# Turning u for the channel layers: by TensorE, or by the transposing DMA in 16-bit halves

## The chip, the cores and the metric

The kernel runs on one core of a Trainium2 chip. The metric is the device time of one execution in microseconds (us), as the median of three runs. A profiled run beside them gives the trace and a page of tables; its span, from the first to the last instruction, is 864.8 us.

The engines of the core work side by side and meet through semaphores: TensorE (PE in the tables, its weight loads PEld), VectorE (DVE), ScalarE (ACT), GpSimd (POOL), and SyncE (SP), which here issues nearly all transfers. A line number such as L584 is a line of the kernel before.

## The reference

Two blocks in a row: routed attention, then a mixer with a token layer and a channel layer. Only the second matters here.

```python
def _moe_ref(x, w_tok1, w_tok2, w_ch1, w_ch2):     # x: (4, 768, 512), the attention's output
    xt = x.transpose(0, 2, 1)
    h = np.maximum(xt @ w_tok1, 0.0) @ w_tok2      # w_tok1: (768, 256), w_tok2: (256, 768)
    u = x + h.transpose(0, 2, 1)
    h2 = np.maximum(u @ w_ch1, 0.0) @ w_ch2        # w_ch1: (512, 1536), w_ch2: (1536, 512)
    return (u + h2).astype(np.float32)
```

All arrays are fp32. `u` has 768 tokens by 512 channels for each of 4 batches.

## The kernel before

In SBUF, `xs[b]` holds u of batch b with tokens on the 128 partitions: `[128, 6, 512]`, six blocks of 128 tokens. The product `u @ w_ch1` sums over channels, so it needs u with channels on the partitions. That is what `turn_u` makes: `uT`, in two halves of 384 tokens (n) by four blocks of 128 channels (f). Each of the eight (n, f) blocks takes three transposes of 128x128 on TensorE into PSUM, and one copy to SBUF, on ScalarE and VectorE in turn.

```python
def turn_u(b, n):
    if n == 0:
        pools["uT"] = pools["u"].tile([P, 2, NF, HS], F32, name="uT")       # HS = 384, NF = 4
        pools["uTs"] = pools["u"].tile([P, 3, NF // 2, HS], F32, name="uTs")
    uT, uTs = pools["uT"], pools["uTs"]
    for f in range(NF):
        pt = pools["ps_m"].tile([P, HJ, P], F32, tag="YZ"[f % 2], name="pt")
        for i in range(HJ):                                                  # HJ = 3
            nc.tensor.transpose(                                             # L584
                out=pt[:, i], in_=xs[b][:, HJ * n + i, f * P : (f + 1) * P], identity=ident
            )
        copy = nc.vector.tensor_copy if f % 2 else nc.scalar.copy
        copy(out=uT[:, n, f], in_=pt.rearrange("p i t -> p (i t)"))          # L588
    if n == 1:
        R = {"B11": uT[:, 0, 0:2], "B21": uT[:, 0, 2:4], "B22": uT[:, 1, 2:4]}
        R["T1"], R["T2"], R["T4"] = (uTs[:, i] for i in range(3))
        R["T3"] = b12 = uT[:, 1, 0:2]
        sub(R["T1"], b12, R["B11"])          # on VectorE, 128x768 each, L535
        sub(R["T2"], R["B22"], R["T1"])
        sub(R["T3"], R["B22"], b12)
        sub(R["T4"], R["B21"], R["T2"])
        pools["R"] = R
```

The sums T1 to T4 are there because both channel layers use the seven-product scheme of Strassen and Winograd: a chunk of a layer is seven products over blocks and sums of blocks instead of eight over blocks.

```python
def chunk(n, product, done, last=False):
    X = ptile("X")
    product(X, "A11", "B11", True)
    if late:
        late.pop()()                     # the last product of the chunk before (A22, T4; c21)
    done("p1", X)                        # first layer: ScalarE copies X to SBUF
    Z = ptile("Z")
    product(Z, "S1", "T1", True)
    done("p5", Z)                        # first layer: ScalarE copies Z
    Y = ptile("Y")
    ...                                  # product(Y, "A12", "B21", True); done("c11", Y)
    product(X, "S2", "T2", False)        # accumulates onto X, which must have been copied
    done("u2", X)
    ...                                  # product(Z, "S4", "B22", False); done("c12", Z)
    product(X, "S3", "T3", False)
    done("c22", X)
    ...                                  # product(X, "A22", "T4", False); done("c21", X): put into late
```

`done` adds on VectorE and, in the first layer (`ch1_chunk`, products at L656), copies (L664) and takes the relu (L668, L675, L688) on ScalarE; in the second (`ch2_chunk`, products at L707) all of it is on VectorE (L538). `ptile` has two buffers for each of X, Y and Z.

The main loop over batches, and the token layers (`ends`, L512 and L521) ahead of it, between which the first batch is turned:

```python
while ends:                               # products of the token layers, with weight work beside them
    ...
    ends.pop(0)()
    if len(ends) in (11, 9):
        turn_u(0, len(ends) == 9)
...
for b in range(B):
    for part in range(2):
        for i in range(3):
            ch1_chunk(part, i)
            ...
        for i in range(3):
            ...
            ch2_chunk(b, part, i)
            if part == 1 and i < 2 and b + 1 < B:
                turn_u(b + 1, i)
        ...
```

Of the kernel before, what the change touches and what calls it, by code (L numbers as in the profile page):

```python
# [8 lines left out]
F32 = mybir.dt.float32  # L9
BF16 = mybir.dt.bfloat16  # L10
U32 = mybir.dt.uint32
I32 = mybir.dt.int32
ALU = mybir.AluOpType
ACT = mybir.ActivationFunctionType
# [2 lines left out]
B, H, S, D = 4, 8, 768, 64  # L17
C = 16
P = 128
NJ = S // P  # L20
DM = H * D
NF = DM // P
# [4 lines left out]
HJ = NJ // 2  # L27
HS = HJ * P
# [19 lines left out]
def kernel(  # L48
# [29 lines left out]
    nc = tc.nc  # L78
# [30 lines left out]
    pools = {}  # L109


    ident = const.tile([P, P], F32, name="ident")
# [15 lines left out]
    xs = [xpool.tile([P, NJ, DM], F32, name=f"x{b}") for b in range(B)]  # L128
# [51 lines left out]
    def weight_steps(pool, W, names):  # L180
# [8 lines left out]
        def tmp(name, dt, n):  # L189
            bufs = 1 if name == "wT" else 2  # L190
            return pool.tile([P, WMAX], dt, tag=name, name=name, bufs=bufs)[:, 0:n]

        def load_bits(src, p):
            n = p["n"] = src.shape[1]
            raw = pool.tile([P, WMAX, 2], U32, tag="raw", name="raw", bufs=3)[:, 0:n]
            nc.sync.dma_start(raw.rearrange("p n two -> p (n two)"), src.bitcast(U32))
            p["lo"], p["hi"] = raw[:, :, 0], raw[:, :, 1]

        def scalar_part(p):

            p["h"] = tmp("wh", U32, p["n"])
            nc.scalar.activation(out=p["h"].bitcast(F32), in_=p["hi"].bitcast(F32), func=ACT.Abs)
            p["up"] = tmp("wup", I32, p["n"])
            nc.scalar.activation(out=p["up"], in_=p["lo"], func=ACT.Copy, scale=float(2.0**-29))

        def rest(dst, p):
# [10 lines left out]
            )  # L217
            T = tmp("wT", U32, p["n"])
            nc.vector.scalar_tensor_tensor(  # L219
                out=T, in0=p["hi"], scalar=0xC0000000, in1=h,  # L220
                op0=ALU.bitwise_and, op1=ALU.bitwise_or,
            )
            T, up = T.bitcast(I32), p["up"]
            if len(dst.shape) == 3:
                T, up = (y.rearrange("t (p j) -> t p j", j=NJ) for y in (T, up))
            nc.gpsimd.tensor_tensor(out=dst.bitcast(I32), in0=T, in1=up, op=ALU.add)  # L226

# [15 lines left out]
    def centroids_norm(cen):  # L243
# [9 lines left out]
        nc.vector.tensor_scalar(  # L253
            out=nrm.bitcast(I32), in0=lo.bitcast(I32), scalar1=0.5, scalar2=float(0x1FBB6875),
            op0=ALU.mult, op1=ALU.add,
# [251 lines left out]
    def tok1(b, t):  # L507
        if t == 0:
            h1s[b] = tokpool.tile([P, NT, DM], F32, name="h1", bufs=2)
        pf = mtile([P, DM], "ph1")  # L510
        for j in range(NJ):
            nc.tensor.matmul(  # L512
                pf, lhsT=W["tok1"][:, j, t * P : (t + 1) * P], rhs=xs[b][:, j],
                start=(j == 0), stop=(j == NJ - 1),
            )
        relu(h1s[b][:, t], pf)
# [17 lines left out]
    def sub(dst, a, b):  # L534
        nc.vector.tensor_tensor(out=dst, in0=a, in1=b, op=ALU.subtract)  # L535

    def add(dst, a, b):
        nc.vector.tensor_tensor(out=dst, in0=a, in1=b, op=ALU.add)  # L538

    def left_weights():  # L540

        w = W["ch1"]
        half = DCH // 2
        A = {
            f"A{i + 1}{j + 1}": w[:, 2 * j : 2 * j + 2, half * i : half * i + half]
            for i in range(2)
            for j in range(2)
        }
        extra = pools["wsums"].tile([P, 3, 2, half], F32, name="w1s")
        A["S1"], A["S2"], A["S4"] = (extra[:, i] for i in range(3))  # L550
        yield lambda: add(A["S1"], A["A21"], A["A22"])
        yield lambda: sub(A["S2"], A["S1"], A["A11"])
        yield lambda: sub(A["A21"], A["A11"], A["A21"])
        yield lambda: sub(A["S4"], A["A12"], A["S2"])
        A["S3"] = A["A21"]
        pools["A"] = A
# [15 lines left out]
        B_["T3"] = B_["B12"]  # L572
        pools["B"] = B_

    def turn_u(b, n):

        if n == 0:
            pools["uT"] = pools["u"].tile([P, 2, NF, HS], F32, name="uT")
            pools["uTs"] = pools["u"].tile([P, 3, NF // 2, HS], F32, name="uTs")
        uT, uTs = pools["uT"], pools["uTs"]  # L580
        for f in range(NF):
            pt = pools["ps_m"].tile([P, HJ, P], F32, tag="YZ"[f % 2], name="pt")
            for i in range(HJ):
                nc.tensor.transpose(  # L584
                    out=pt[:, i], in_=xs[b][:, HJ * n + i, f * P : (f + 1) * P], identity=ident
                )
            copy = nc.vector.tensor_copy if f % 2 else nc.scalar.copy
            copy(out=uT[:, n, f], in_=pt.rearrange("p i t -> p (i t)"))  # L588
        if n == 1:
            R = {"B11": uT[:, 0, 0:2], "B21": uT[:, 0, 2:4], "B22": uT[:, 1, 2:4]}  # L590
            R["T1"], R["T2"], R["T4"] = (uTs[:, i] for i in range(3))
            R["T3"] = b12 = uT[:, 1, 0:2]
            sub(R["T1"], b12, R["B11"])
            sub(R["T2"], R["B22"], R["T1"])
            sub(R["T3"], R["B22"], b12)
            sub(R["T4"], R["B21"], R["T2"])
            pools["R"] = R

    late = []

# [42 lines left out]
    def ch1_chunk(part, i):  # L643

        c = 3 * part + i
        if i == 0:
            pools["h2"] = {
                k: pools["mlp"].tile([P, 3, HS], F32, name="h" + k)
                for k in ("A11", "A12", "A22", "S1", "S2", "S3", "S4")
            }  # L650
        A, R, h2 = pools["A"], pools["R"], pools["h2"]
        kept = {}

        def product(psum, a, r, start):
            for k in range(2):
                nc.tensor.matmul(  # L656
                    psum, lhsT=A[a][:, k, c * P : (c + 1) * P], rhs=R[r][:, k],
                    start=start and k == 0, stop=k == 1, skip_group_check=not start,
                )

        def done(name, psum):
            if name in ("p1", "p5", "u2"):
                kept[name] = pools["mlp"].tile([P, HS], F32, name=name, bufs=2)
                nc.scalar.copy(out=kept[name], in_=psum)  # L664
            elif name == "c11":
                a = h2["A11"][:, i]
                add(a, psum, kept["p1"])
                nc.scalar.activation(out=a, in_=a, func=ACT.Relu)  # L668
            elif name == "c12":
                kept["c12"] = pools["mlp"].tile([P, HS], F32, name="c12", bufs=2)  # L670
                add(kept["c12"], psum, kept["u2"])
            elif name == "c22":
                a = h2["A22"][:, i]
                add(a, psum, kept["p5"])
                nc.scalar.activation(out=a, in_=a, func=ACT.Relu)  # L675

                nc.vector.scalar_tensor_tensor(
                    out=h2["S3"][:, i], in0=kept["c12"], scalar=0.0, in1=h2["A11"][:, i],
                    op0=ALU.max, op1=ALU.subtract,
                )  # L680
                nc.vector.scalar_tensor_tensor(
                    out=h2["S1"][:, i], in0=kept["c12"], scalar=0.0, in1=a,
                    op0=ALU.max, op1=ALU.add,
                )
                sub(h2["S2"][:, i], h2["S1"][:, i], h2["A11"][:, i])
            else:
                a = h2["A12"][:, i]
                nc.scalar.activation(out=a, in_=psum, func=ACT.Relu)  # L688
                sub(h2["S4"][:, i], a, h2["S2"][:, i])

        chunk(HS, product, done)
# [34 lines left out]
    good = const.tile([P, 3], F32, name="good")  # L726
    count = const.tile([1, 3], I32, name="count")

# [77 lines left out]
    ends = [lambda t=t: tok1(0, t) for t in range(NT)]  # L806
# [73 lines left out]
    pools["wsums"] = pool("wsums", 1, side="right")  # L880
    pools["u"] = pool("upool", 1, side="right")
    beside = weights + list(left_weights())
    while ends:
        for _ in range(-(-len(beside) // len(ends))):
            beside.pop(0)()
        ends.pop(0)()
        if len(ends) in (11, 9):
            turn_u(0, len(ends) == 9)
    staging.close()
    tokens.close()  # L890
    pools["mlp"] = pool("mlp", 1)
# [1 line left out]
    for b in range(B):  # L893
        for part in range(2):
            for i in range(3):
                ch1_chunk(part, i)
                for _ in range(2):
                    if beside:
                        beside.pop(0)()
            for i in range(3):  # L900
                if b == B - 1 and part == 1 and i == 2:
                    both = fits_load()
                ch2_chunk(b, part, i)
                if part == 1 and i < 2 and b + 1 < B:
                    turn_u(b + 1, i)
            if b == 0:
                (fits_count if part else fits)()
    late.pop()()
# [212 lines left out]
```

## Time and profile before

| | us |
|---|---|
| device time, median of three runs | 867.04 (866.88 to 867.43) |
| span of the profiled run | 864.8 |
| TensorE clock granted | 0.998 of full speed |

The stages, read from the trace: attention up to about 330 us, the token layers up to 416 us, and the channel layers of four batches from there to the end. The groups of instructions that turn u (columns: line, engine, operation, out<-in, shape, count; then busy us in all and mean ns of one; then the idle time of the engine just before them and what ended it):

```profile
L584 PE MATMUL pt<-ident,x 128*128 128x128 f32 x96 | 11.8, 273 | 0.0
L588 DVE COPY uT<-pt 128x384 f32<-128x384 f32 x16 | 8.9, 558 | 2.2 <-PE pt L584 1.4
L588 ACT COPY uT<-pt 128x384 f32<-128x384 f32 x16 | 7.7, 480 | 53.1 <-PE pt L584 53.1
L535 DVE TENSOR_TENSOR uTs<-uT,uTs 128x768 f32<-128x768 f32 x8 | 7.6, 955 | 0.4
```

The mean of one transpose, 273 ns, includes the fill of a pipeline in which neighbours overlap; what twelve of them take on the path is read from the chain of work that ended last, in order of time. Busy time is the union of an engine's instructions. An engine's idle time costs something only where the engine is on that chain.

### The profile page before, as it was taken

What the parts mean: (1) busy time and instruction counts of PE and PEld (TensorE: products, weight loads), DVE (VectorE), ACT (ScalarE), POOL (GpSimd) and SP (SyncE); (2) the same over time, 40 slices, a digit from 0 to 9 for tenths busy, and PEclk for the clock granted to TensorE, in tenths of its full rate; (3) what the DMA queues carried; (4) which work ended last, traced back from release to release, by engine and by line L of the source; (5) the groups of instructions that cost most, each with busy time, mean ns of one, the idle gap of its engine ahead of it and who ended that gap; (6) DMA issues with size and microseconds to landing.
All of it is one profiled execution on the core that took longest, in us unless ns stands there. A gap on an engine that the chain in (4) does not pass through costs nothing.

```text
span 864.8 us, 11041 instructions
## 1 busy us (share of the span) xinstructions
PE 856.0 (99%) x4294; PEld 525.0 (61%) x4294; DVE 511.0 (59%) x864; ACT 290.7 (34%) x490; POOL 45.8 (5%) x40
## 2 busy tenths in 40 slices
PE   9999999999999999999999999999999999999997
PEld 4444444444444444445578586685876867768676
DVE  6878887989898861896553444423444334443342
ACT  5566566566666651321210311203112021120210
POOL 1001010101101000330000000000000000000000
PEclk9999999999999999999999999999999999999999
DMA  9855455666564300420000010000010000100001
GB/s 148 150 122 114 92 116 112 126 99 137 113 128 105 87 25 0 145 75 1 0 1 1 0 38 37 0 1 0 25 49 1 0 1 25 49 1 1 0 14 64
DMA packets 133276, 47.62 MB, mean 55 GB/s; under 512 B 122080, under 2 KB 126176, under 8 KB 133216
## 3 DMA queue, kind: packets, MB, share of 16 engines
q1 hardware_dynamic: 131616, 46.45, 24.2%
q8 instruction: 35, 0.57, 0.3%
q10 hardware_dynamic: 1600, 0.39, 0.2%
q14 instruction: 25, 0.20, 0.1%
HBM read 34.64 MB, written 6.29 MB: 47 GB/s over the span
## 4 chain that ended last, share of the span: by engine, by line
PE 94%; DVE 4%; issue 0%; DMA 0%; DVEq 0%; ACT 0%
PE sc L420 18%; PE pX L707 14%; PE pX L656 14%; PE av L443 14%; PE pZ L707 7%; PE pZ L656 7%; PE ph L512 4%; PE pY L707 4%; PE pY L656 4%; PE pu L521 3%; PE px L472 1%; PE small L459 1%; PE pt L584 1%; PE small L301 1%; DVE wh L214 1%; DVE wT L219 1%
## 5 line engine op out<-in xcount | busy, mean ns | idle before, releaser
L425 ACT ACTIVATE ex<-sc 128x768 f32<-128x768 f32 x192 | 151.4, 812 | 71.1 <-PE av L443 36.5
L420 PE MATMUL sc<-qkT 64*128 64x384 f32 x768 | 155.1, 482 | 0.0
L433 DVE TENSOR_TENSOR sum<-sum,ex 128x768 f32<-128x768 f32 x128 | 127.7, 998 | 28.3 <-ACT ex L425 15.6
L443 PE MATMUL av<-ex,va 128*64 128x384 f32 x768 | 127.4, 488 | 0.0
L443 PEld LDWEIGHTS av<-ex,va 128*64 128x64 f32 x768 | 53.7, 137 | 71.8 <-issue 69.9
L420 PEld LDWEIGHTS sc<-qkT 64*128 64x128 f32 x768 | 67.9, 187 | 39.4 <-issue 39.4
L656 PE MATMUL pX<-uT,wc 128*128 128x384 f32 x192 | 67.4, 487 | 0.0
L420 PE MATMUL sc<-ohT 64*128 64x384 bf16 x384 | 62.7, 323 | 0.2 <-DVE ohT L393 0.2
L664 ACT COPY p<-pX 128x384 f32<-128x384 f32 x24 | 11.4, 475 | 150.0 <-PE pX L656 150.0
L656 PEld LDWEIGHTS pX<-uT,wc 128*128 128x128 f32 x192 | 36.2, 190 | 24.7 <-issue 1.0
L226 POOL TENSOR_TENSOR wc<-wT,wup 128x512 int32<-128x512 int32 x24 | 33.1, 1378 | 199.9 <-DVE wT L219 199.9
L512 PE MATMUL ph<-x,wt 128*128 128x512 f32 x96 | 42.1, 594 | 0.8 <-DVE x L524 0.8
L521 PE MATMUL pu<-h,wt 128*128 128x512 f32 x96 | 42.0, 592 | 0.0
L538 DVE TENSOR_TENSOR c<-pZ,u 128x384 f32<-128x384 f32 x24 | 13.4, 558 | 46.8 <-PE pZ L656 46.8
L420 PEld LDWEIGHTS <-ohT 64*128 64x128 bf16 x384 | 18.6, 94 | 33.2 <-issue 9.4
L538 DVE TENSOR_TENSOR hA<-pY,p 128x384 f32<-128x384 f32 x24 | 13.4, 557 | 40.1 <-PE pY L656 40.1
L538 DVE TENSOR_TENSOR x<-pX,x 128x256 f32<-128x256 f32 x24 | 10.2, 424 | 42.6 <-PE pX L707 42.6
L707 PE MATMUL pX<-w2s,hS 128*128 128x256 f32 x144 | 35.2, 380 | 0.0
L707 PE MATMUL pX<-wc,hA 128*128 128x256 f32 x144 | 35.0, 379 | 0.0
L707 PE MATMUL pZ<-w2s,hS 128*128 128x256 f32 x144 | 35.0, 379 | 0.0
L707 PE MATMUL pY<-wc,hA 128*128 128x256 f32 x144 | 35.0, 379 | 0.0
L707 PE MATMUL pX<-w2s,hA 128*128 128x256 f32 x144 | 35.0, 379 | 0.0
(127 smaller groups left out, 1173.4 us busy)
## 6 DMA issues: line engine op xcount, KB each, us to landing
raw<-in_moe_w_ch_dram SPq DMA_DIRECT2D x24, 512.0 KB, 4.1
va<-in_v_dram SPq DMA_DIRECT2D x16, 384.0 KB, 3.3
out_dram<-x SPq DMA_DIRECT2D x24, 256.0 KB, 2.0
qk<-in_k_dram SPq DMA_DIRECT2D x60, 96.0 KB, 4.0
qk<-in_q_dram SPq DMA_DIRECT2D x60, 96.0 KB, 3.6
raw<-in_moe_w_tok_dram SPq DMA_DIRECT2D x3, 512.0 KB, 4.4
raw<-in_moe_w_tok_dram SPq DMA_DIRECT2D x4, 384.0 KB, 4.0
ex<-in_q_dram ACTq DMA_DIRECT2D x4, 96.0 KB, 3.3
```

What stands on the lines that cost most here:

```text
L214: nc.vector.tensor_scalar(out=h, in0=h, scalar1=0x07FFFFFF, scalar2=3, op0=ALU.bitwise_and, op1=ALU.logical_shift_left,)
L226: nc.gpsimd.tensor_tensor(out=dst.bitcast(I32), in0=T, in1=up, op=ALU.add)
L420: nc.tensor.matmul(sc[:, h, 0:HS], lhsT=src[rows, 1, j], rhs=src[rows, 0, js], start=start, stop=not start,)
L425: nc.scalar.activation(out=ex, in_=sc[:, :, 0:HS], func=ACT.Exp, scale=SM_SCALE)
L433: nc.vector.tensor_tensor(out=acc, in0=acc if j > 1 else st["ex", qh, 0], in1=st["ex", qh, j], op=ALU.add)
L443: nc.tensor.matmul(av[h * D : (h + 1) * D], lhsT=st["va"][:, h, j], rhs=ex[:, h], start=(j == 0), stop=(j == NJ - 1),)
L512: nc.tensor.matmul(pf, lhsT=W["tok1"][:, j, t * P : (t + 1) * P], rhs=xs[b][:, j], start=(j == 0), stop=(j == NJ - 1),)
L521: nc.tensor.matmul(pu, lhsT=W["tok2"][:, t, j], rhs=h1s[b][:, t], start=(t == 0), stop=(t == NT - 1))
L538: nc.vector.tensor_tensor(out=dst, in0=a, in1=b, op=ALU.add)
L656: nc.tensor.matmul(psum, lhsT=A[a][:, k, c * P : (c + 1) * P], rhs=R[r][:, k], start=start and k == 0, stop=k == 1, skip_group_check=not s ...
L664: nc.scalar.copy(out=kept[name], in_=psum)
L707: nc.tensor.matmul(psum, lhsT=h2[a][:, k, i * P : (i + 1) * P], rhs=Bw[w][:, 3 * part + k], start=start and k == 0, stop=k == 2, skip_grou ...
```

## The change

u is turned by the DMA that transposes as it moves, instead of by TensorE. That DMA moves elements of 16 bits, so each fp32 block is taken apart into its low and high halves, both are turned, and the halves are put together again. Bits are only moved: the numbers stay the same.

For each of the eight (n, f) blocks of a batch:
- a *take*: ScalarE copies 128 x 3 x 128 fp32 numbers, seen as 16-bit words, into `urows`, low halves first and high halves behind them (128x768 words);
- a transposing DMA, issued from ScalarE's own queue, turns the six 128x128 blocks of `urows` into `ucols`;
- a *put*: ScalarE copies the halves from `ucols` into the interleaved words of `uT`.

It is meant to take work off TensorE and VectorE and to use ScalarE and the DMA engines, which have time in the later stages.

```diff
+    def u_take(b, i):
+
+        n, f = divmod(i, NF)
+        x = xs[b][:, HJ * n : HJ * n + HJ, f * P : (f + 1) * P].bitcast(U16)
+        rows = pools["u"].tile([P, 2, HJ, P], U16, name="urows", bufs=2)
+        nc.scalar.copy(out=rows, in_=x.rearrange("p j (c w) -> p w j c", w=2))
+        cols = pools["u"].tile([P, 2, HJ, P], U16, name="ucols", bufs=2)
+        nc.scalar.dma_start_transpose(
+            out=cols.rearrange("p w j t -> p (w j) t"),
+            in_=rows.rearrange("p w j c -> p (w j c)"),
+        )
+        pools["ucols", i] = cols
+
+    def u_put(i):
+        n, f = divmod(i, NF)
+        if i == 0:
             pools["uT"] = pools["u"].tile([P, 2, NF, HS], F32, name="uT")
...
+        out = pools["uT"][:, n, f].bitcast(U16).rearrange("p (t w) -> p w t", w=2)
+        nc.scalar.copy(out=out, in_=pools.pop(("ucols", i)).rearrange("p w j t -> p w (j t)"))
+
+    def u_steps(b):
+
+        N = 2 * NF
+        yield lambda: (u_take(b, 0), u_take(b, 1))
+        for i in range(N):
+            yield lambda i=i: (u_put(i), i + 2 < N and u_take(b, i + 2))
+
+    def u_sums():
...                                       # T1 to T4 as before, now in a step of their own
```

The steps stand in the main loop as follows. Batch 0 is turned between the products of the token layers; its sums come after the last of them. For the other batches, the first two takes come behind the second chunk of the first channel layer's second part, the rest behind the first chunk of the second channel layer, and the sums behind its last chunk.

```diff
+    turning = list(u_steps(0))
     while ends:
...
         ends.pop(0)()
-        if len(ends) in (11, 9):
-            turn_u(0, len(ends) == 9)
+        if len(ends) < 17 and turning:
+            turning.pop(0)()
+    u_sums()
...
                 ch1_chunk(part, i)
+                if (part, i) == (1, 1) and b + 1 < B:
+                    turning = list(u_steps(b + 1))
+                    turning.pop(0)()
...
                 ch2_chunk(b, part, i)
-                if part == 1 and i < 2 and b + 1 < B:
-                    turn_u(b + 1, i)
+                if part == 1 and i == 0:
+                    while turning:
+                        turning.pop(0)()
+            if part == 1 and b + 1 < B:
+                u_sums()
```

On each engine the instructions keep the order in which the code records them. On ScalarE the first two takes of a batch, each with its DMA issue behind it, therefore stand between the relu of c22 and the relu of c21 of that chunk, ahead of the copy of the next chunk's X.

More of the change, by code (lines that the diff above doesn't have):

```diff
@@ L11 @@
 U32 = mybir.dt.uint32
+U16 = mybir.dt.uint16
 I32 = mybir.dt.int32
@@ L573, in right_weights @@
         pools["B"] = B_
-    def turn_u(b, n):
-        if n == 0:
-            pools["uT"] = pools["u"].tile([P, 2, NF, HS], F32, name="uT")
[L579 to L597, printed above, removed]
+    def u_take(b, i):
[9 more added lines that the diff above has]
+        pools["ucols", i] = cols
@@ L599 @@
+    def u_sums():
+        uT = pools["uT"]
+        uTs = pools["uTs"] = pools["u"].tile([P, 3, NF // 2, HS], F32, name="uTs")
+        R = {"B11": uT[:, 0, 0:2], "B21": uT[:, 0, 2:4], "B22": uT[:, 1, 2:4]}
+        R["T1"], R["T2"], R["T4"] = (uTs[:, i] for i in range(3))
+        R["T3"] = b12 = uT[:, 1, 0:2]
+        sub(R["T1"], b12, R["B11"])
+        sub(R["T2"], R["B22"], R["T1"])
+        sub(R["T3"], R["B22"], b12)
+        sub(R["T4"], R["B21"], R["T2"])
+        pools["R"] = R
     late = []
```

## The prediction

> **What bounds the kernel now.** I read the page's busy shares first, then the chain of work that ended last.
>
> ```profile
> PE 856.0 (99%) x4294; PEld 525.0 (61%) x4294; DVE 511.0 (59%) x864; ACT 290.7 (34%) x490; POOL 45.8 (5%) x40
> ...
> PE 94%; DVE 4%; issue 0%; DMA 0%; DVEq 0%; ACT 0%
> PE sc L420 18%; PE pX L707 14%; PE pX L656 14%; PE av L443 14%; PE pZ L707 7%; PE pZ L656 7%; PE ph L512 4%; PE pY L707 4%; PE pY L656 4%; PE pu L521 3%; PE px L472 1%; PE small L459 1%; PE pt L584 1%; PE small L301 1%; DVE wh L214 1%; DVE wT L219 1%
> ```
>
> TensorE sets the end: it is busy 99% of the span and is 94% of the chain, at a granted clock of 0.998. Every TensorE microsecond taken out counts, as long as no new wait opens. What the change takes out is `pt L584`, 1% of the chain. So the prize is known before anything else: about 1%.
>
> Next, the same chain in order of time, between batch 0 and batch 1 (start, length, what):
>
> ```profile
> 504.32 1.29 PE pX L707 x6
> 505.62 1.31 PE pt L584 x12
> 506.93 2.59 PE pX L707 x12
> ...
> 516.00 1.31 PE pt L584 x12
> ...
> 522.49 1.36 PE pX L707 x6
> ```
>
> Twelve transposes take 1.31 us between two products, without a gap on either side: the matrix work waits for them and for nothing else. One product of either layer is 1.29 us.
>
> Then what ScalarE does in this stage, first by its longest wait (engine and line, what it waited for: total, times, longest):
>
> ```profile
> ACT p L664 <- PE pX L656: 150.0, 8, 25.4
> ```
>
> and then by its timeline in the chunk of the first channel layer in which the changed kernel will put the first two turns:
>
> ```profile
> 488.16 0.52 ACT L675 ACTIVATE hA<-hA 128x384 f32<-128x384 f32 x1 [2.69 <-DVE hA L538]
> 490.14 0.49 ACT L688 ACTIVATE hA<-pX 128x384 f32<-128x384 f32 x1 [1.47 <-PE pX L656]
> 490.53 0.47 ACT L664 COPY p<-pX 128x384 f32<-128x384 f32 x1
> 491.49 0.48 ACT L664 COPY p<-pZ 128x384 f32<-128x384 f32 x1 [0.49 <-PE pZ L656]
> ```
>
> ScalarE sleeps up to 25.4 us while the second channel layer runs, so there is a large hole. But inside the first channel layer its holes are 1.5 to 2.7 us, and `p<-pX` at 490.53 is needed soon: the accumulation onto that X starts on TensorE at 492.52 and may not start before X was copied.
>
> Last, the only transposing DMA of the kernel before, that of the one-hots (12 blocks of 128x128 in 16 bits, issued by SyncE):
>
> ```profile
> L346 SPq DMA_TRANSPOSE ohT<-oh x15: 1324/1474/1627, 23.9 to 293.2; - x15
> ...
> DMA to landing us min/median/max: 3.7/3.8/5.5
> ```
>
> It holds the issuing queue for 1.47 us and lands after 3.8 us. All 15 are issued by 293.2, before u exists, so the two kinds don't meet.
>
> **What the Trainium skill says.** "DMA: Bandwidth & Descriptors", section "DMA Transpose (X-bar)": the transposing DMA takes 2-byte elements only and is issued from SyncE or ScalarE. That is why fp32 is split in halves; the trace has only the 16-bit case. "Perfetto Trace Analysis", section "Per-instruction lifecycle": the window shown for such a DMA is the generation of its descriptors, during which the issuing sequencer takes no next instruction. The trace agrees: 1.47 us of issue against 3.8 us to landing, and at the start four plain DMAs on ScalarE's queue (2.08 us) stand ahead of its first work. "ScalarE: Activation LUTs", section "What ACT_TABLE_LOAD costs": one element per cycle and lane, 186 ns + 0.833 ns each, fp32 and bf16 alike: 826 ns for 768. The trace has 812 ns for the exponential of 128x768 out of PSUM, and 684 ns for 128x512 read from SBUF at a stride of two words. Nothing here shows 16-bit integers at stride two; I take 0.88 us, from 684 + 256 x 0.833 = 897, less a little for the overlap of neighbours.
>
> **What is removed.** Eight groups of 12 transposes. The chain gives 1.33 us for each of the two in batch 0's stage and 1.31 for the other six: 10.5 us. With them go 16 copies out of PSUM (ACT 480 ns, DVE 558 ns), beside TensorE except for one thing: before, VectorE's copies and sums of u in the middle of the second layer delay `p`, and TensorE waits 0.07 us (the 1.36 above) in each of three batches, 0.2 us. Together 10.7 us, all on the path.
>
> **What is added.** Per batch 8 takes and 8 puts of 128x768 16-bit elements on ScalarE, 16 x 0.88 = 14.1 us, 56 us in all, and 8 DMA issues on its queue. Each transfer has half the blocks of `ohT`; between half its issue (0.74) and the whole (1.47) I take 1.1 us, and 3 us to landing. Where does this lie?
>
> (a) Batch 0, beside the token layers. ScalarE's last weight step ends at 378, the relu it owes TensorE comes due at 392.8. Five takes and three puts stand before it: 8 x 0.88 + 5 x 1.1 = 12.5 us, ending near 391. No wait. The rest, 3 takes and 5 puts, ends about 406; the layer begins at 416 - 2.7 = 413. Hidden.
>
> (b) The four sums of u (0.95 us each) now follow VectorE's last addition of the token layer instead of coming 13 us earlier. That addition starts 0.2 after the last token product and takes 0.69, T1 takes 0.95: 1.84 us. TensorE has only one product (1.29) before it needs T1. A new wait of 0.6 us, once. For the other batches two products (2.58) lie ahead of T1 and the addition is 0.42 us, so T1 is there after 1.6: no wait. T2 follows 0.96 later and is needed two products later.
>
> (c) Batches 1 to 3, the other six takes and eight puts, behind the last relu of the first channel layer, beside the second. Three chunks of 7 products are 21 x 1.29 = 27.1 us; the last relu ends 3.3 us into them. The first product with T2, the last to need a put, starts four products (5.2 us) after them, and T2 itself takes 0.96: some 28 us. Need: a step of put, take and issue is 0.88 + 0.88 + 1.1 = 2.9; six of them 17, the last two puts with one landing 3: 20 us. The dependent loop (put, take, landing, two in flight) is 0.88 + 0.88 + 3 = 4.8 per two steps, less than the 5.7 of ScalarE's own work, so latency doesn't show. Hidden, 8 us to spare.
>
> (d) Batches 1 to 3, the first two takes, in the middle of the first channel layer. They come after the relu of c22 that ends at 488.7, ahead of the relu at 490.14 and of `p<-pX`. Each take 0.88, 0.15 until the DMA sees it (estimate from the 0.16 to 0.2 us steps between engines in the timeline), issue 1.1: two make 4.3, to 493.0. The relu (0.49) and the copy (0.47) then end at 493.95, and the product that waits started at 492.52 before. So TensorE waits about 1.4 us, three times: 4.2 us. Once paid, ScalarE has caught up: `p<-pZ` is due 1.29 later and takes 0.48.
>
> Sum: 867.0 - 10.7 + 0.6 + 4.2 = 861.1. Because ScalarE's neighbours overlap a little and the issue may be nearer its half, I say 860.8.
>
> **The rivals.**
> 1. *All of it hidden.* If the issue costs 0.74 us or less, (d) shrinks to 0.7 x 3 or vanishes: 867.0 - 10.7 + 0.6 = 857 us. For: the transfer is half as large; plain issues on ScalarE's queue took 0.52 us each. Against: `ohT` varies by only 20% around 1.47, so part of the cost may be fixed.
> 2. *ScalarE becomes the bound* in the stages between batches. If a 16-bit copy at stride two runs at half speed (1.6 us), (c) needs 6 x 4.3 + 5 = 31 us against 28, and (d) grows by 1.5 us: 3 to 4 us more per batch, 866 to 872 us. For: no run here shows such an operand. Against: reads at a stride of two words, `wh<-raw`, show hardly a penalty (566 ns for 128x384, 684 for 128x512: 0.92 ns per element).
> 3. *Latency of the turn dominates.* If two transfers of ScalarE's queue run one after the other, or landing takes 5.5 us (the worst of `ohT`), a pair of steps is 7.3 us and (c) ends at about 26 us: still in time. It would take 6 us and more to show. The DMA engines are under 10% busy there, so I give it little.
>
> **Range and chances.** The removal is sure to 0.3 us. Only (d) is wide: 0 to 2.3 us a batch, 0 to 7 in all, and rival 2 adds a tail upward. 857.3 to 865.5 us should hold it 8 times in 10. Faster by over 2% means under 849.7, 7 us more than all that is removed: 1%. Slower by over 2% (over 884.4) needs ScalarE to be late by 27 us: 2%. Within 2%: 97%.
>
> **What would show it.** `pt` gone from the chain and no `uT` copies on VectorE; PE busy near 846. Rows of `urows` (takes) and `uT<-ucols` (puts) on ScalarE at 0.88 us and its busy time near 340; rows of a transposing DMA on ScalarE's queue at about 1.1 us. In the chain, a step of ScalarE, `urows` or `p<-pX`, three times for about 1.4 us in the second part of the first channel layer, and 0.6 us of VectorE's `uTs` where that layer first begins. No step of `ucols` or of a DMA at the start of a batch. The prediction is wrong if ScalarE's 16-bit copies are well over 1 us, if `uT` or T1 is late at the start of batches 1 to 3, or if the wait in (d) is missing.

## The result and the profile after

| | before | after |
|---|---|---|
| device time, median of six runs each, us | 866.88 (866.64 to 867.43) | 860.46 (860.20 to 861.28) |
| ratio | | 0.9927, 95% interval 0.9914 to 0.9940 |
| span of the profiled run, us | 864.8 | 858.4 |

The change saves 6.4 us, 0.7%: less than the 10.7 us that the prediction takes off the path. The page of the kernel after shows what was exchanged, in the busy times and in the shares of the chain that ended last:

```profile
PE 846.0 (99%) x4198; PEld 514.9 (60%) x4198; DVE 502.2 (59%) x848; ACT 338.5 (39%) x538; POOL 45.7 (5%) x40
...
PE 92%; DVE 5%; ACT 1%; ACTq 1%; issue 0%; DMA 0%; DVEq 0%
```

TensorE lost 96 instructions and 10 us; ScalarE gained 48 us. The chain, which had less than 1% of ScalarE and nothing of its queue before, now has 1% of each. (Line numbers are those of the kernel that ran: in the kernel after, the first layer's products are L674 and its copies L682, the second layer's products L725, a take is L583, its DMA issue L585 and a put L596; an edit shifts them by a line or two.) Where that share lies is seen in the same chain in order of time, in the first channel layer of batch 0 (start, length, what):

```profile
485.21 0.57 DVE hA L539
485.78 0.02 issue
485.81 0.52 ACT hA L693
486.33 0.73 ACT urows L583
487.06 0.02 issue
487.08 1.23 ACTq L585
488.31 0.04 issue
488.35 0.84 ACT urows L583
489.19 0.02 issue
489.21 1.23 ACTq L585
490.44 0.05 issue
490.49 0.49 ACT hA L706
490.98 0.38 ACT p L682
491.35 0.04 issue
491.40 1.56 PE pX L674 x4
```

Read it from the end. The product at 491.40 waited for the copy `p` of X. That copy stood behind a relu, the relu behind the two takes (`urows`) and their two DMA issues, and these behind the relu of c22. It is the path of part (d) of the prediction. TensorE's own timeline of the stage has the length of the wait:

```profile
488.88 1.45 PE L674 MATMUL pY<-uT,wc 128*128 128x384 f32 x4
491.40 1.56 PE L674 MATMUL pX<-uTs,w1s 128*128 128x384 f32 x4 [1.06 <-ACT p L682]
492.79 1.45 PE L674 MATMUL pZ<-uT,w1s 128*128 128x384 f32 x4
```

Without a wait the product would start 1.29 us after the one before it, at 490.17. It starts 1.23 us later and then takes 0.1 us longer to get going. The list of waits counts three of these, one for each of batches 1 to 3, and the one for T1 at the start of the channel layers (engine and line, what it waited for: total, times, longest):

```profile
PE pX L674 <- ACT p L682: 3.2, 3, 1.1
...
PE pZ L674 <- DVE uTs L536: 0.4, 1, 0.4
```

The sizes of the new steps, from the view of the tiles `urows` and `ucols` (count, then shortest/median/longest in ns):

```profile
L583 ACT COPY urows<-x x32: 814/819/832, 377.5 to 734.8; 128x768 uint16<-128x768 uint16 x32
L585 ACTq DMA_TRANSPOSE ucols<-urows x32: 1227/1228/1808, 378.4 to 735.6; - x32
...
L596 ACT COPY uT<-ucols x32: 1037/1053/1059, 381.9 to 738.4; 128x768 uint16<-128x768 uint16 x32
...
DMA to landing us min/median/max: 2.8/2.8/4.0
```

A take is 0.82 us, a put 1.05, an issue 1.23, and a turn lands after 2.8. Behind the last relu of the first channel layer, ScalarE's timeline has the puts for batch 1, with the other six takes and issues between them, from 498.55 to 519.66, 21.1 us almost without a gap, and then nothing until the copy of the next batch's first X:

```profile
518.61 1.05 ACT L596 COPY uT<-ucols 128x768 uint16<-128x768 uint16 x1 [0.46 <-DMA ucols<-urows]
524.37 0.48 ACT L682 COPY p<-pX 128x384 f32<-128x384 f32 x1 [4.70 <-PE pX L674]
```

### The profile page after: what moved, and what is told of

Read it like the earlier page. It is cut to its first block, busy times and chain, and to the rows that moved or that the text cites. A ratio compares the mean times of both kernels' runs of the same rounds, so it can differ in the third digit from the quotient of the medians.

```text
span 858.4 us, 10914 instructions
## 1 busy us (share of the span) xinstructions
PE 846.0 (99%) x4198; PEld 514.9 (60%) x4198; DVE 502.2 (59%) x848; ACT 338.5 (39%) x538; POOL 45.7 (5%) x40
## 4 chain that ended last, share of the span: by engine, by line
PE 92%; DVE 5%; ACT 1%; ACTq 1%; issue 0%; DMA 0%; DVEq 0%
PE sc L421 18%; PE pX L725 14%; PE av L444 14%; PE pX L674 14%; PE pZ L725 7%; PE pZ L674 7%; PE ph L513 4%; PE pY L725 4%; PE pY L674 3%; PE pu L522 3%; PE px L473 1%; PE small L460 1%; PE small L302 1%; DVE wh L215 1%; ACTq L585 1%; DVE wT L220 1%
## 5 line engine op out<-in xcount | busy, mean ns | idle before, releaser
L674 PE MATMUL pX<-uT,wc 128*128 128x384 f32 x192 | 67.4, 487 | 0.0
L682 ACT COPY p<-pX 128x384 f32<-128x384 f32 x24 | 11.4, 475 | 123.8 <-PE pX L674 116.2
L674 PEld LDWEIGHTS pX<-uT,wc 128*128 128x128 f32 x192 | 36.2, 190 | 24.7 <-issue 1.0
L596 ACT COPY uT<-ucols 128x768 uint16<-128x768 uint16 x32 | 33.7, 1052 | 35.2 <-issue 23.0
L539 DVE TENSOR_TENSOR c<-pZ,u 128x384 f32<-128x384 f32 x24 | 13.4, 558 | 47.8 <-PE pZ L674 47.8
L674 PE MATMUL pX<-uTs,w1s 128*128 128x384 f32 x96 | 35.2, 489 | 3.2 <-ACT p L682 3.2
L693 ACT ACTIVATE hA<-hA 128x384 f32<-128x384 f32 x24 | 12.6, 523 | 63.5 <-DVE hA L539 63.5
L451 ACT COPY avT<-av 128x384 f32<-128x384 f32 x32 | 15.4, 480 | 52.3 <-PE av L444 52.3
L674 PE MATMUL pZ<-uTs,w1s 128*128 128x384 f32 x96 | 35.0, 487 | 0.4 <-DVE uTs L536 0.4
L725 PE MATMUL pX<-w2s,hA 128*128 128x256 f32 x144 | 35.0, 379 | 0.0
```

What stands on the lines that cost most here:

```text
L451: nc.scalar.copy(out=st["avT"][:, js].rearrange("p j t -> p (j t)"), in_=av)
L596: nc.scalar.copy(out=out, in_=pools.pop(("ucols", i)).rearrange("p w j t -> p w (j t)"))
L674: nc.tensor.matmul(psum, lhsT=A[a][:, k, c * P : (c + 1) * P], rhs=R[r][:, k], start=start and k == 0, stop=k == 1, skip_group_check=not s ...
L725: nc.tensor.matmul(psum, lhsT=h2[a][:, k, i * P : (i + 1) * P], rhs=Bw[w][:, 3 * part + k], start=start and k == 0, stop=k == 2, skip_grou ...
```

## The experiments

The theory: the change takes 10.7 us off TensorE's path and gives back 4.2 us in two kinds of new wait, 3.7 us behind the first two takes and 0.5 us for T1; all else is hidden. The rivals: the transposing traffic or ScalarE's work costs TensorE something as such, or u comes late. Each ratio is to runs of the kernel before on the same chip.

**Do the two waits hold all that was lost?** Four kernels on one chip. The first moves the two takes behind the last relu of that layer; the second moves the sums of batch 0; the third does both; the fourth leaves the takes where they are and lets SyncE issue the DMAs.

```diff
 first, takes later:
-                if (part, i) == (1, 1) and b + 1 < B:
-                    turning = list(u_steps(b + 1))
-                    turning.pop(0)()
...
-                if part == 1 and i == 0:
-                    while turning:
-                        turning.pop(0)()
+                if part == 1 and i == 0 and b + 1 < B:
+                    for step in u_steps(b + 1):
+                        step()
 second, sums early (the third has both):
             turning.pop(0)()
-    u_sums()
+        if len(ends) == 4:
+            u_sums()
 fourth, issued by SyncE:
-        nc.scalar.dma_start_transpose(
+        nc.sync.dma_start_transpose(
```

> The first two takes of batches 1 to 3 moved behind the last relu of the first channel layer, to the other six. Theory (the lost time is ScalarE's two takes and two DMA issues standing ahead of the copy of X): the three waits of 1.23 us on that copy vanish, 860.5 - 3.7 = 856.8 us; the last put ends about 3 us later against the product that needs it, still in time. Rival (the transposing traffic itself or a late u costs the time): no gain or a loss, 860 to 866 us, since the last put now comes later.

> Only the four sums of u of batch 0 moved ahead, to four token products before the end. Theory: the wait of 0.5 us for T1 vanishes, 860.0 us, and nothing else moves. Rival (that half microsecond is the start-up of the layer and stays): 860.5 us.

> Both moves together. Theory: the two waits are on one engine's chain and add up, 860.5 - 3.7 - 0.5 = 856.3 us, 10.7 us under the kernel before, which is all that the removed transposes took. Rival: something of the 10.7 us is held back elsewhere, 857.5 us or more.

> The takes stay where they are, but SyncE issues their DMAs. Theory: what stands ahead of the copy of X falls from 4.2 us (two takes of 0.82 and two issues of 1.23) to 1.6 us, below the 3.0 us of room there, so no wait: 856.8 us. Rival (the copies are what delays, by their access to u or to the same memory): the wait stays or shrinks in proportion to the takes' 1.6 of 4.2 us, 858 us or more. A danger for both: SyncE's queue also carries the output, behind which the later transfers may stand; over 860 us if that makes u late.

| kernel | us | ratio to before (95%) |
|---|---|---|
| takes later | 856.84 | 0.9884 (0.9869 to 0.9899) |
| sums early | 860.29 | 0.9924 (0.9911 to 0.9938) |
| both | 856.13 | 0.9877 (0.9862 to 0.9892) |
| issued by SyncE | 856.96 | 0.9885 (0.9870 to 0.9900) |

With the takes later, the three waits on `p` are gone from the list and the time is 856.8, as expected. The rival falls: the last put now ends 0.3 us ahead of the sum T2 that needs it (523.4 against 523.66), where it was 4.5 ahead, and costs nothing:

```profile
522.34 1.06 ACT L596 COPY uT<-ucols 128x768 uint16<-128x768 uint16 x1 [0.46 <-DMA ucols<-urows]
523.66 0.96 DVE L536 TENSOR_TENSOR uTs<-uT,uTs 128x768 f32<-128x768 f32 x1
```

TensorE's timeline of that kernel in the place of the wait has no gap:

```profile
489.71 1.45 PE L674 MATMUL pY<-uT,wc 128*128 128x384 f32 x4
491.00 1.45 PE L674 MATMUL pX<-uTs,w1s 128*128 128x384 f32 x4
```

With SyncE issuing, the copies stay and the issues go, and the wait goes too. So it is not what the takes touch, but how long ScalarE is held ahead of `p`: 4.25 us of takes and issues did it, 1.6 us of takes alone doesn't. SyncE's queue did hold later turns back behind an output, the put there waits 5.1 us for its DMA, and that too was hidden.

The sums alone are too small for whole times. Their kernel is 0.2 us faster than the kernel after, which lies within the runs of either; the part ahead of the channel layers, which the edit hardly touches, starts those layers anywhere from 412.9 to 414.1 us in these traces. From the first product with `uT` to the last, it is 410.8 us in the kernel after, 410.2 with the sums early, 406.8 with the takes later and 406.2 with both: 0.6 and 4.0 us, which add up. In the kernel before it is 414.3: 8.1 us more than with both moves, which is what the prediction has in this stretch (six groups of transposes at 1.31 us and three waits of 0.07). The list of waits agrees: that on `uTs` is gone with the sums early.

Both together, 856.13 us, is the fastest version that was run: 10.7 us under the 866.80 us of the kernel before on that chip.

**Is there a hidden cost besides?** One kernel leaves turning and sums of batches 1 to 3 out and lets them use the u of batch 0.

```diff
-                if (part, i) == (1, 1) and b + 1 < B:
-                    turning = list(u_steps(b + 1))
-                    turning.pop(0)()
...
-                if part == 1 and i == 0:
-                    while turning:
-                        turning.pop(0)()
-            if part == 1 and b + 1 < B:
-                u_sums()
```

> Turning and sums of batches 1 to 3 are left out; these batches use the u of batch 0, so the numbers are not the reference's. This is the time when the turn costs nothing after batch 0. Theory: only the 3.7 us of waits go, 856.8 us, the same as with the takes moved. Rival (the turn costs TensorE something more, through memory or DMA): below 856 us.

856.59 us, ratio 0.9881 (0.9863 to 0.9899): the same as with the takes later, 0.9884, though whole times can't tell apart less than about 2 us by these intervals. The stretch from the first product with `uT` to the last is sharper: 406.8 us in both. With the takes later, then, turning three batches by DMA costs TensorE less than 0.1 us. The rival of a cost by traffic falls.

**How much room is there ahead of the copy of X?** Either one take of the two is moved away, or both copies run twice (in batches 1 to 3).

```diff
 one take:
-        yield lambda: (u_take(b, 0), u_take(b, 1))
+        yield lambda: u_take(b, 0)
+        yield lambda: u_take(b, 1)
 takes twice:
-    def u_take(b, i):
+    def u_take(b, i, times=1):
...
-        nc.scalar.copy(out=rows, in_=x.rearrange("p j (c w) -> p w j c", w=2))
+        for _ in range(times):
+            nc.scalar.copy(out=rows, in_=x.rearrange("p j (c w) -> p w j c", w=2))
...
-        yield lambda: (u_take(b, 0), u_take(b, 1))
+        yield lambda: [u_take(b, i, 2 if b else 1) for i in range(2)]
```

> Only one take with its issue stays in the middle of the first channel layer, the second goes to the others. Theory (ScalarE has 3.0 us of room ahead of the copy of X, everything over it is a wait of TensorE): 2.1 us of work is under the room, no wait, 856.8 us. Rival (the wait is in proportion to what stands there): half of it stays, 858.6 us.

> In batches 1 to 3 the copies of the first two takes run twice, 2 x 0.73 = 1.5 us more work ahead of the copy of X. Theory: the whole of it is on the path, 1.2 + 1.5 = 2.7 us of wait, 860.5 + 4.4 = 864.9 us. Rival (in proportion: 1.23 us per 4.25): 860.5 + 1.3 = 861.8 us.

One take: 856.84 us, ratio 0.9883 (0.9867 to 0.9900), no wait on `p`. There is a threshold and no proportion: 2.1 us of work is free, 4.25 us costs 1.23.

Takes twice: 870.62 us (869.4 to 872.4), ratio 1.0048 (1.0031 to 1.0064), slower than the kernel before. Above the threshold all of it counts (the waits below), so the rival falls, but it came out 5.7 us over what I expected. Its timeline of TensorE, in batch 0 and then in batch 2:

```profile
489.72 1.45 PE L675 MATMUL pY<-uT,wc 128*128 128x384 f32 x4
493.96 2.26 PE L675 MATMUL pX<-uTs,w1s 128*128 128x384 f32 x4 [2.79 <-ACT p L683]
496.02 2.48 PE L675 MATMUL pZ<-uT,w1s 128*128 128x384 f32 x4
498.34 1.45 PE L675 MATMUL pX<-uT,wc 128*128 128x384 f32 x4
```

```profile
720.76 1.56 PE L675 MATMUL pX<-uTs,w1s 128*128 128x384 f32 x4 [2.79 <-ACT p L683]
```

The wait is 1.72 us longer than in the kernel after (I had 1.5: a copy repeated onto the same tile takes 0.86 us more and not 0.73). And in two of the three batches, 0 and 1, the products behind it are slow. Stretches of batch 0 give the cause (us, then busy time of PE, PEld, DVE, ACT and POOL with counts, then the granted clock, the DMA share and GB/s):

```profile
493.90:496.20 2.30, 2.24 (x5) 1.34 (x6) 0.70 (x2) 0.92 (x3) 0.00 (x0) 0.67 0.03 5
496.20:498.40 2.20, 2.20 (x6) 1.16 (x5) 0.00 (x0) 0.48 (x1) 0.00 (x0) 0.57 0.00 0
498.40:500.00 1.60, 1.60 (x7) 1.04 (x6) 0.73 (x2) 0.00 (x0) 0.00 (x0) 1.00 0.00 0
```

The clock fell just after the wait, and 1.7 us were lost on two products. The slices of 0.67 and 0.57 average over its edges: in slices of 0.02 us it is at 0.50 from 494.67 to 498.09, and in batch 1 (1.5 us lost) from 607.31, 0.3 us before the wait ended, to 610.73: 3.41 us each. The 1.06 us of the kernel after left it at 1.00. The Trainium skill, "TensorE: Matmul & The Clock Gate", section "Part 1: The HAM clock gate (the "warmup" mystery)", says that the clock falls to half after an idle window of about 3.4 us and comes back after as long a busy one. The half and the way back fit. The first part fits only if a window need not be idle throughout, since these waits are shorter than one.

The trace shows why the third wait was spared. Counted from the fall at 494.67, the other three edges are 1, 33 and 34 steps of 3.413 us later, so they lie on one grid. In the step that ends at 494.67 TensorE was idle for 2.7 us, in the one that ends at 607.31 for 2.5. The wait of batch 2, from 717.97 to 720.76, is cut by the grid at 719.95 into 2.0 and 0.8 us. The kernel with the puts three times, below, agrees: its edges lie on a grid of the same step (in batch 2 at 651.00, 654.41, 657.82 and 664.65), its five falls end steps with 2.3 to 3.4 us of idleness, and a wait of 3.48 us that the grid cuts into 2.0 and 1.5, up to 529.59, left the clock at 1.00. So in these two traces it is the idle part of a fixed step that decides, the limit lying between 2.0 and 2.3 us of 3.4, and where a wait falls on the grid is chance. That may also be why two of the four executions, at 871.8 and 872.4 us, are over 2 us longer than the others and have a mean clock of 0.991 to 0.992 against 0.996; they have no trace.

**How much room is there beside the second channel layer?** In batches 1 to 3 each put runs two or three times; and, in all batches, each put is followed by a plain copy of the same size.

```diff
 twice (or 3 in place of 2):
-    def u_put(i):
+    def u_put(i, times=1):
...
-        nc.scalar.copy(out=out, in_=pools.pop(("ucols", i)).rearrange("p w j t -> p w (j t)"))
+        cols = pools.pop(("ucols", i)).rearrange("p w j t -> p w (j t)")
+        for _ in range(times):
+            nc.scalar.copy(out=out, in_=cols)
...
-            yield lambda i=i: (u_put(i), i + 2 < N and u_take(b, i + 2))
+            yield lambda i=i: (u_put(i, 2 if b else 1), i + 2 < N and u_take(b, i + 2))
 plain copy:
+        pools["urows", i] = rows
...
-        nc.scalar.copy(out=out, in_=pools.pop(("ucols", i)).rearrange("p w j t -> p w (j t)"))
+        cols = pools.pop(("ucols", i))
+        nc.scalar.copy(out=out, in_=cols.rearrange("p w j t -> p w (j t)"))
+        nc.scalar.copy(out=pools.pop(("urows", i)), in_=cols)
```

> In batches 1 to 3 each put runs twice, about 8 x 0.93 = 7.4 us more of ScalarE's work beside the second channel layer. Theory (some 8 us to spare there): the last put ends just about when the sums need it, 860.5 to 862 us. Rival (ScalarE's work costs in these stages as it is, since it shares something with TensorE): 3 us or more.

> Each put three times: 14.9 us more per batch. Theory: the room of about 8 us is used up and the rest, some 7.5 us, is a wait of TensorE before the product with T2, three times: about 883 us. Rival (in proportion): twice what the doubled puts cost.

> Each put is followed by a copy of the same 128x768 16-bit elements out of ucols into urows, both sides without a stride, to see why a put takes 1.05 us and a take 0.82. If the put's strided write costs the 0.23 us, the plain copy takes about 0.82; if 1.05 us comes from reading what the DMA wrote, it takes 1.05. The added 5.8 to 7.5 us per batch fit in the room: about 860.5 us.

| kernel | us | ratio to before (95%) |
|---|---|---|
| puts twice | 866.09 | 0.9987 (0.9981 to 0.9994) |
| puts three times | 896.65 | 1.0338 (1.0320 to 1.0355) |
| plain copy added | 860.91 (one run) | |

The plain copies lengthen a step from 3.04 to 3.90 us, 6.9 us in a batch, and cost next to nothing: the stretch from the first product with `uT` to the last is 410.9 us, against 410.8 in the kernel after. So ScalarE's work beside the second layer is free as such, and the rival of a shared cost falls, though the time of the doubled puts alone, over 5 us above the kernel after, would have spoken for it. There my expectation missed. A doubled put, 2.14 us, lengthens a step by 1.09 us and not by 0.93, so a batch has 8.7 us more and not 7.4. The chain of that kernel shows what the last microsecond does:

```profile
527.57 1.06 ACT uT L598
528.63 0.02 issue
528.66 0.96 DVE uTs L536
...
530.40 0.95 DVE uTs L536
...
531.41 0.33 DVE x L539
531.74 0.48 DVE hA L539
532.22 0.02 issue
532.24 0.52 ACT hA L688
532.76 0.38 ACT u L684
533.14 0.04 issue
533.18 4.14 PE pX L676 x12
```

The late put delays T2, and with it T3 and T4; behind them stand an addition of VectorE's for the second layer, that for c11, its relu on ScalarE, and the copy `u`, for which TensorE waits again. One delay is paid at two products. From the product Y to the late product five places on, 1.5 to 1.8 us are lost in each batch, 5.0 in all. Where I had 8 us of room, there were 7.3: in batch 1, counted from the start of the channel layers, the last put ends 7.8 us later than in the kernel after, and the product with T2 is 0.56 late; with the plain copies it ends 6.2 us later, and no product is late. A put that is half a microsecond or so too late costs two to three times that, because the order of the queues hands the delay on.

With the puts three times it is 36 us where I had 22.5, and far over twice the cost of the doubled ones, so neither the theory nor the rival has the number. Waits for T1 stand beside those for T2 that I expected:

```profile
PE pX L676 <- DVE uTs L536: 13.1, 3, 5.5
...
PE pZ L676 <- DVE uTs L536: 11.1, 4, 3.6
```

A step is 2.16 us longer than in the kernel after, 17.3 us in a batch and not 14.9. By the starts of the products, the two waits of a batch hold TensorE up by 8.1 to 9.3 us, 26.2 in all; the other 10 us are almost all products slowed while the clock was at 0.50. The mechanism was right, each put over the room being a wait, but the step was mis-sized by 0.3 us and the clock was left out.

Of the plain copy the trace has this:

```profile
L599 ACT COPY urows<-ucols x32: 816/820/840, 383.5 to 745.3; 128x768 uint16<-128x768 uint16 x32
```

It reads what the DMA wrote, as the put does, and writes without a stride (and into another tile). So it is not the read, and by all that is left the write of 16-bit words at a stride of two, that makes a put 0.23 us longer; a take, which reads at that stride, is at 0.82 as well.

## Why the prediction was right

860.8 us were predicted, 860.46 measured, within the range. TensorE is busy 846.0 us (846 was said), ScalarE 338.5 (340). The mechanism held step by step, but that the number is so close is partly luck: in (d) the errors cancel, and the last 0.3 us were taken off the sum of 861.1 with the thought that the issue may be nearer its half, which it was not. By its steps:

- **Removed, 10.7 us.** Shown by the version with both moves, 10.67 us under the kernel before (866.80 - 856.13; 9.4 to 12.0 by its interval). Had the new work cost much besides, that version couldn't have got all of it back. (The copies out of PSUM that went are 16 on each of two engines, 32 and not 16; they were off the path but for the 0.2 us that those on VectorE helped to cost.)
- **(a) Batch 0 hidden.** The fifth take's issue ends at 390.96 where 391 was said, though the work ahead of it took 13.4 us and not 12.5 and began 0.5 us earlier. The relu runs at 392.5, as soon as its product is there, and the last put ends at 404.7, ahead of the layer at 412.9.
- **(b) A wait of 0.6 us for T1.** The product Z starts at 414.74, where without a wait it would have been at 412.93 + 1.29 = 414.22: 0.52 us, and 0.6 in the sum with the sums moved.
- **(c) Batches 1 to 3 hidden.** 21.1 us instead of 20, and 7.3 us of room instead of 8. A put was mis-sized, 1.05 us for 0.88, and a step of put, take and issue is 3.04 us and not 2.9; the latency of the turn showed only ahead of the last put, by 0.46.
- **(d) Three waits of 1.4 us, 4.2 in all.** 1.23 us each with 0.1 us of restart, 4.0 in all. Two takes with their issues last 4.25 us where 4.3 was said, but only because the sizes erred in opposite senses: the issue is 1.23 us and not 1.1, a DMA issue follows its copy after 0.02 us and not 0.15, and a take is 0.82 and not 0.88.

Of the rivals, "all of it hidden" (857 us) is what the moved takes reach, and failed here because half the blocks do not halve the issue: 1.23 us for 6 blocks against 1.47 for 12. "ScalarE becomes the bound" and "latency" did not occur. What no step of the prediction had is the fall of the clock behind a longer wait; at 1.2 us per wait the clock stayed at 1.00.

## What to carry to other kernels

Work moved to an engine that is mostly idle is free only where it stands behind everything that the busy engine still awaits in that stretch: the idle share of ScalarE was 61%, and still three pairs of takes with their issues cost 4 us, because each stood ahead of one copy with 3 us of room; moved behind the last relu they cost nothing. Count the issue of a DMA as time of the engine that issues it. And find the room of each stage from the timeline, since beyond it every microsecond counts, and is paid more than once where queues on several engines follow each other or where the wait is long enough for the clock to fall.

## What the runs showed of the hardware that was not expected

- A transposing DMA of six 128x128 blocks of 16 bits holds ScalarE's queue for 1.23 us and SyncE's for 1.21; one of twelve blocks holds SyncE's for 1.47. A line through the two gives, as an estimate, about 1 us and 0.04 us a block. To landing it is 2.8 and 3.8 us.
- A ScalarE copy of 128x768 16-bit words takes 0.82 us plain or read at a stride of two, and 1.05 us written at a stride of two.
- TensorE's clock changed between 1.00 and 0.50 on a grid of 3.413 us in two traces. It fell at the end of a step in which TensorE had idled 2.3 us or more, seven times, and stayed at 1.00 where the grid cut a wait of 2.79 or 3.48 us into parts of at most 2.0 us. It was at 0.50 for one step or two.
